# Rounding weight blocks two behind, and moving two small jobs behind the chain stages, in an attention-plus-MLP kernel

## The chip, the cores and the metric

The kernel runs on one core of a Trainium2 chip. The metric is the device time of one execution in microseconds (us); lower is better. Three runs of the kernel before gave 793.99, 795.82 and 796.3 us, with 795.82 us as the median. The profile and the trace come from one more execution, which took 794.06 us.

## The reference

A recurrent attention runs over 768 tokens for 4 batches of 8 heads with 40 elements each, and its output goes through a two-layer MLP (called moe in the code):

```python
for t in range(S):                       # S = 768, per batch and head
    y[t]  = r[t] @ state                 # state is 40 x 40
    Sa    = state @ a[t]
    state = state * w[t][:, None] - outer(Sa, b[t]) + outer(v[t], k[t])
x = y.transpose(0, 2, 1, 3).reshape(3072, 320)
h = x @ w_in                             # 320 x 2048, given as float64
g = where(h >= 1, h, where(h <= -1, 0, (h + 1)**2 / 4))
out = g @ w_out                          # 2048 x 320, given as float64
```

## The kernel before, in words

**Attention.** The 768 tokens are cut into 24 chunks (`c`) of 32 tokens, and the 32 heads into two halves (`hb`). One chunk and half has a generator `chain(c, hb)` with four stages, called one at a time by `stage(c, hb)`. The first stage multiplies scores with values and state (L519) and copies the result on ACT (L523). The second multiplies with the inverse of the chunk's triangular matrix (L529) and writes it back in four pieces on DVE (L536) and four on ACT (L540); the two engines swap PSUM tiles halfway, and the profile shows DVE's third piece waiting for ACT's pieces and ACT's third for DVE's. The third makes the new state and the output (L545 to L568), and the fourth the last product (L585, L587). Then `round_y` (L575 on ACT, L576 on POOL) splits the output into a rounded part and a rest in the tile `Y`.

**MLP.** When two chunks are done, `relayout` issues six DMAs on SP (L605 to L614) that bring `Y` into `X`, and the generator `moe` runs 64 tokens of all batches: `first` (L637, tile `ph`), `gate` (L647 and L648 on ACT, L650 on DVE, L653 on ACT, L654 on POOL) and `second` (L668). The first group starts in the fourth quarter of chunk 2's step.

**Weights.** The float64 weights are converted on the chip in 28 blocks: 12 of `w_in`, then 16 of `w_out`. `weights()` is a generator in which a block takes three pulls: in the first ACT writes the two tiles `x` (L751) and `low` (L755); in the second the block before is rounded by `split` (L771 on ACT, L772 on POOL or DVE); in the third DVE joins `x` and `low` (L759). `split(k)` also issues the load of raw block `k + 5` (L739) on SP's queue for `w_out`. Blocks of `w_out` have three places for `x` and one for `low`, all in `tiab`.

**Order.** The program is one hand-written order; each engine and each queue runs its own part of it in order. One step of the main loop (L923 on) handles a chunk in four quarters. Each quarter calls the stages that are ready, hands out turns and loads, and then calls `fill`, which interleaves six portions of MLP matmuls, of weight pulls (0.8 a portion in the first two steps, then 1) and of background work for later chunks (rows, pair products and inverses, with their own windows). In the second and fourth quarter, `shift` (two copies on ACT, L310) prepares the transposed columns that `turn` (L464, L467, L469 on DVE) takes up later. In those two quarters the order on ACT is: the two copies of `shift`, the fourth stage's `round_y`, then the four pieces L540 of the other half's second stage.

Of the kernel before, what the change touches and what calls it, by code (L numbers as in the profile page):

```python
# [55 lines left out]
def rwkv_moe_kernel(ctx: ExitStack, tc: tile.TileContext, r, k, v, w, a, b, w_in, w_out, ident_d, mask_d, out):  # L56
# [30 lines left out]
    tiab = const.tile([128, 16, 80], F32, name="tiab")  # L87
# [25 lines left out]
    pairs_f = pairs.rearrange("p m i -> p (m i)")  # L113
# [22 lines left out]
    def copy_rv(s, part, c, n=1):  # L136

        x, o = ((r, O_R), (v, O_V))[part]
        nc.sync.dma_start(
            scr[s][0 : NH * 128].rearrange("(h x) e -> h x e", x=128)[:, L * c : L * (c + n), o : o + D],  # L140
            x.rearrange("b h t e -> (b h) t e")[:, 128 * s + L * c : 128 * s + L * (c + n), :],
        )

    flat = lambda x: x.rearrange("p a e -> p (a e)")
# [227 lines left out]
    def adopt(s):  # L372

        drain("inv", s)
        W = lw[:, 1024:2048]
        nc.vector.transpose(tinv.rearrange("p c h i -> p i (c h)"), W.rearrange("p (a i) -> p i a", i=32))
        turned_out.add(s)
# [33 lines left out]
    def background(n):  # L411

        due = []
        for key in ("inv", "ab", "rows"):
            for s in range(1, NS):
                a, b = window(key, s)
                if a < n <= b:
                    drain(key, s - 1)
                    at = spent.setdefault((key, s), [0])
                    due.append((key, s, at, size[key] * (gone(n) - gone(a)) / (gone(b) - gone(a))))  # L420
        while True:
            due = [(k, s, at, to) for k, s, at, to in due if done[k] < s and at[0] < to]
            if not due:
                return
            key, _, at, _ = max(due, key=lambda x: x[3] - x[2][0])
            at[0] += next(back[key])
# [3 lines left out]
    def load_ti(c, hb):  # L430
        drain("rows", c // 4)
        tis[c, hb] = tih[hb]
        load_rows(tih[hb], c, 0, 200, 16 * hb, 16)
# [20 lines left out]
    def shift(c, hb):  # L454
        shift_rows(tis[c, hb])
# [15 lines left out]
    def scores(c, hb, parts=(0, 1)):  # L471
        u = 2 * c + hb
        for part in parts:
            (score_products, score_masks)[part](u)
# [29 lines left out]
    def chain(c, hb):  # L504
# [11 lines left out]
        for h in range(16):  # L516
            f, p = h % 2, h // 2
# [8 lines left out]
        for h in range(16):  # L526
            f, p = h % 2, h // 2
# [26 lines left out]
        for h in range(16):  # L554
            f = h % 2
# [18 lines left out]
        def round_y():  # L574
            nc.scalar.copy(yv[:, 0], yt)  # L575
            nc.gpsimd.tensor_sub(yv[:, 1], yt, yv[:, 0].bitcast(F32))  # L576

        yield
        if last:
            round_y()  # L580
            return
        psv = psum()[:, 0:256].rearrange("p (h x) -> p h x", x=32)
        for h in range(16):
            f, p = h % 2, h // 2
            nc.tensor.matmul(psv[er[f], p, :], lhsT=ss[er[f], p, :], rhs=pn[er[f], p, 0, 8:40], start=True, stop=True)  # L585
        for f in range(2):
# [1 line left out]
                out=cn[er[f], f::2, C_R : C_R + 32], in0=psv[er[f]], scalar=-1.0,  # L588
                in1=pr[er[f], :, 1, 39:40].broadcast_to([D, 8, 32]), op0=ALU.mult, op1=ALU.mult,
            )  # L590
        round_y()
        yield

    groups = [(t, 64) for t in range(0, S, 64)]
# [131 lines left out]
    def weight_tile(k, t):  # L726
        kind, j, i, _ = jobs[k]
        if kind:
            if w2_pool[j // 8 ^ 1] is None:
                open_w2(j // 8 ^ 1)  # L730
            return w2_pool[j // 8 ^ 1].tile([128, 2, 320], t, name=f"w2_{j}", tag=f"w2_{j}")
        return w1_tile(j, i, t)

    def raw_load(k):
        raws[k] = weight_tile(k, F32).rearrange("p b n -> p (b n)")
        x, at = raws[k].bitcast(I32), 0
        for src in jobs[k][3]:
            m = src.shape[0]
            (nc.sync if jobs[k][0] else nc.gpsimd).dma_start(x[at : at + m], src.bitcast(I32))  # L739
            at += m  # L740

    def weights():

        def start(k):
            m, n = sizes[k]
            words = raws[k][0:m]
            if jobs[k][0]:
                x, low = (flat(tiab)[0:m, n * i : n * i + n] for i in (k % 3, 3))
            else:
                x, low = (Xraw[y][0:m, n * i : n * i + n] for y, i in (((1, 1), (0, 0), (1, 0), (0, 1))[k % 4], (1 - k % 2, 2)))  # L750
            nc.scalar.activation(  # L751
                x, words.rearrange("p (n b) -> p n b", b=2)[:, :, 1], AF.Prelu, scale=2.0**-112, alpha=2.0**32
            )
            low = low.bitcast(U32)
            nc.scalar.activation(  # L755
                low, words.bitcast(U8).rearrange("p (n b) -> p n b", b=8)[:, :, 3], AF.Copy, bias=-15.5 / 32, scale=1.0 / 32
            )
            yield
            nc.vector.scalar_tensor_tensor(  # L759
                out=x.bitcast(U32), in0=x.bitcast(U32), scalar=3, in1=low,  # L760
                op0=ALU.logical_shift_left, op1=ALU.bitwise_or,
            )
            yield x

        def split(k, x):
            m, n = sizes[k]
            kind, j, i, _ = jobs[k]
            del raws[k]
            wt[kind, j, i] = new = weight_tile(k, F32R)
            hi, lo = (new[0:m, p] for p in range(2))  # L770
            nc.scalar.copy(hi, x)  # L771
            (nc.gpsimd if kind or k < 7 else nc.vector).tensor_sub(lo, x, hi.bitcast(F32))  # L772
            converted[0] = k + 1
            if (kind, i) == (0, 2):
                wb = new.bitcast(F32)
                for q in range(2):
                    nc.gpsimd.dma_start(wb[80:120, q], wb[40 * q : 40 * q + 40, 0])
            if 12 <= k + AHEAD < len(jobs):
                raw_load(k + AHEAD)

        late = None
        for k in range(len(jobs)):
            s = start(k)
            next(s)
            yield
            if late:
                split(*late)
            yield
            late = k, next(s)
            yield  # L790
        split(*late)

    def pull(gen, n=1):
        for _ in range(n):
            if next(gen, "end") == "end":
                return False
        return True
# [45 lines left out]
    load_cg(0, 1)  # L843
    for i in range(2):
        copy_rv(0, i, 1)
    gens = {}

    def stage(c, hb):

        if (c, hb) in gens:  # L850
            next(gens[c, hb], 0)

    def turn_1(j, part):
        early_evict(1, j, part, early_turn(1, j, part))
# [13 lines left out]
    at(14, lambda: load_ti(1, 0))  # L868
    at(38, lambda: scores(0, 0, (1,)))
    gens[0, 0] = chain(0, 0)  # L870
    at(40, lambda: stage(0, 0))
    for half in range(2):
        at(41 + half, lambda half=half: early_ab(1, half))
    at(58, lambda: shift(0, 1))
    i = 0
# [17 lines left out]
    def feed(cols):  # L893

        if not Xs:
            return
        owed[0] += cols * (not idle[0])
        while owed[0] > 0:
            d = next(mgen)
            owed[0] = 0 if d is None else owed[0] - d  # L900
            idle[0] = d is None

    def catch_up():

        for f in deferred:
            f()
        deferred.clear()

    def fill():

        catch_up()
        for k in range(6):
            feed(1280)
            if first:
                first.pop(0)()
            due[0] += PACE[now[0] >= 20]
            while due[0] > 0:
                pull(wgen)
                due[0] -= 1
            background(now[0] + 10 / SLOTS * (k + 1) / 6)  # L920
        now[0] += 10 / SLOTS

    for c in range(NC + 1):  # L923
        nxt = c + 1 < NC
        if c < NC:
            if c:
                gens[c, 0] = chain(c, 0)
            gens[c, 1] = chain(c, 1)
        stage(c - 1, 1)
        if c:  # L930
            stage(c, 0)
        if c < NC:
            if c and c % 4 == 0:
                adopt(c // 4)
            for j in (0, 1) if c else (2, 0, 1):
                turn(c, 1, j)
        fill()
        if nxt:
            shift(c + 1, 0)
        stage(c - 1, 1)  # L940
        stage(c, 0)
        if c < NC:
            scores(c, 1)
        if nxt:
            load_ti(c + 1, 1)
        if nxt:
            load_cg(c + 1, 0)
            turn(c + 1, 0, 2)
        fill()
        for g, (t0, nt) in enumerate(groups):  # L950
            if t0 + nt == 32 * c:
                Xs[g] = relayout(g)
                if idle[0]:
                    owed[0], idle[0] = -TRAIL * 3072, False
        if c == NC:
            break
        stage(c, 0)
        stage(c, 1)
        if nxt:
            for j in (0, 1):  # L960
                turn(c + 1, 0, j)
        fill()
        if nxt:
            shift(c + 1, 1)
        stage(c, 0)
        stage(c, 1)
        if c + 2 < NC:
            load_ti(c + 2, 0)
        if nxt:
            scores(c + 1, 0)  # L970
            load_cg(c + 1, 1)
            turn(c + 1, 1, 2)
        fill()
# [33 lines left out]
```

## Time and profile before

| what | value |
|---|---|
| median of three runs | 795.82 us |
| the profiled execution | 794.06 us |
| its span, from the first to the last instruction | 792.2 us |
| PE busy, share of the span | 679.2 us, 86% |
| DVE | 587.9 us, 74% |
| ACT | 479.6 us, 61% |
| POOL | 444.5 us, 56% |
| mean granted clock of TensorE | 0.910 |

PE is TensorE's matmuls, DVE VectorE, ACT ScalarE, POOL GpSimd, SP SyncE, which issues most DMAs. A wait is idle time of an engine ahead of an instruction, put down to what ended it. The shares are means over stretches with different limits: chunks 0 and 1 have no MLP work, the weight blocks are done by 183 us, and the last instruction of the attention lies near 745 us.

### The profile page before, as it was taken

Reading aid. Unit: us, or ns where it says so; the run is one execution under the profiler, and the core shown is the slowest. Engines: PE = TensorE matmul, PEld = TensorE weight load, DVE = VectorE, ACT = ScalarE, POOL = GpSimd, SP = SyncE. Lnnn points to the kernel's source line nnn. Section 1 sums busy time; section 2 is a strip of 40 time slices with the busy share of each in tenths; the row PEclk is TensorE's granted clock in tenths of the full one; section 3 lists DMA queues with packets and bytes.
Section 4 is the critical chain, followed back from the end, with each engine's and each line's share of the span. In section 5 each row is a group of like instructions: output and inputs, shape, how many; then the busy total and the mean of one; then the engine's idle time right before and its main releaser. Section 6 shows DMA issues by size and latency. Waiting matters only on the chain.

```text
span 792.2 us, 35505 instructions
## 1 busy us (share of the span) xinstructions
PE 679.2 (86%) x15360; PEld 624.1 (79%) x15360; DVE 587.9 (74%) x1329; ACT 479.6 (61%) x1016; POOL 444.5 (56%) x615
## 2 busy tenths in 40 slices
PE   4645557787799888899979899999999999999997
PEld 3534546676788777889878789889999999999996
DVE  6997888778778776987767988778877778776211
ACT  5636756666465565557657466565765666655544
POOL 1232989765236998558657677654476642222332
PEclk9765555889799998899989999999999999999999
DMA  8899966765866566675338564442443324330000
GB/s 299 211 208 188 222 188 181 203 160 145 175 161 171 145 147 142 146 193 110 93 85 189 139 173 94 116 86 45 98 86 83 77 59 96 74 86 20 33 22 18
DMA packets 180523, 102.35 MB, mean 129 GB/s; under 512 B 124760, under 2 KB 172056, under 8 KB 180368
## 3 DMA queue, kind: packets, MB, share of 16 engines
q1 hardware_dynamic: 175216, 83.53, 46.6%
q0 software_dynamic: 4992, 16.39, 7.5%
q8 instruction: 121, 1.98, 1.1%
q14 instruction: 34, 0.28, 0.1%
q10 hardware_dynamic: 160, 0.16, 0.1%
HBM read 70.88 MB, written 27.53 MB: 124 GB/s over the span
## 4 chain that ended last, share of the span: by engine, by line
PE 50%; DVE 9%; DMA 5%; POOL 5%; ACT 4%; issue 3%; SPq 1%; ACTq 0%; DVEq 0%; POOLq 0%
PE ph L637 17%; PE po L668 15%; PE p L556 4%; PE p L585 3%; PE p L545 3%; PE p L485 3%; PE p L529 2%; PE p L519 2%; DMA scr<-arena 2%; DMA tiab<-scr 1%; PE p L336 1%; DVE gt L650 1%; POOL lw L369 1%; POOL gl L654 1%; DVE cg L563 1%
## 5 line engine op out<-in xcount | busy, mean ns | idle before, releaser
L654 POOL TENSOR_TENSOR gl<-gt,gh 128x512 fp32r<-128x512 f32 x95 | 122.0, 1284 | 204.9 <-ACT gh L653 155.7
L637 PE MATMUL ph<-X,w 120*128 120x256 f32 x1536 | 221.3, 297 | 3.1 <-DMA X<-Y 2.8
L637 PEld LDWEIGHTS ph<-X,w 120*128 120x128 f32 x1536 | 199.6, 199 | 11.1 <-issue 3.1
L668 PE MATMUL po<-w,gh 128*128 128x320 f32 x768 | 136.1, 320 | 10.6 <-ACT gh L653 10.0
L668 PEld LDWEIGHTS po<-w,gh 128*128 128x128 f32 x768 | 118.2, 195 | 13.3 <-ACT gh L653 11.8
L653 ACT CAST gh<-gt 128x512 fp32r<-128x512 f32 x95 | 58.8, 619 | 112.4 <-DVE gt L650 103.5
L650 DVE SCALAR_TENSOR_TENSOR gt<-gt,ph 128x512 f32<-128x512 f32 x95 | 65.0, 684 | 79.5 <-ACT gt L648 74.9
L647 ACT ACTIVATE gt<-ph,half_c 128x512 f32<-128x512 f32 x95 | 65.3, 688 | 56.5 <-PE ph L637 55.9
L369 POOL TENSOR_TENSOR lw<-lw 128x31 f32<-128x31 f32 (+15 forms) x155 | 91.6, 591 | 8.4
L536 DVE SCALAR_TENSOR_TENSOR cg<-p,mask 32x128 f32<-32x128 f32 x192 | 55.2, 287 | 48.9 <-ACT cg L540 44.8
L363 POOL TENSOR_TENSOR lw<-lw 128x31 f32<-128x31 f32 (+15 forms) x155 | 81.3, 525 | 7.9
L497 DVE TENSOR_TENSOR cg<-p,mask 32x256 f32<-32x256 f32 x192 | 80.5, 419 | 3.5
L668 PE MATMUL po<-w,gl 128*128 128x320 f32 x384 | 76.0, 321 | 7.1 <-POOL gl L654 7.1
L563 DVE SCALAR_TENSOR_TENSOR cg<-p,pr 40x160 f32<-40x160 f32 x184 | 59.0, 321 | 15.7 <-PE p L556 13.7
L668 PEld LDWEIGHTS po<-w,gl 128*128 128x128 f32 x384 | 62.4, 195 | 9.7 <-POOL gl L654 9.6
L556 PE MATMUL p<-cg 128*64 128x72 f32 (+1 forms) x1536 | 64.4, 241 | 0.0
L648 ACT ACTIVATE gt<-gt 128x512 f32<-128x512 f32 x95 | 60.0, 632 | 3.1
L545 PE MATMUL p<-cg 128*40 128x40 f32 x1472 | 43.9, 218 | 20.1 <-ACT cg L540 19.5
L545 PEld LDWEIGHTS p<-cg 128*40 128x40 f32 x1472 | 37.0, 130 | 30.2 <-ACT cg L540 23.3
L540 ACT ACTIVATE cg<-p 32x160 f32<-32x160 f32 x192 | 56.7, 296 | 6.5 <-DVE cg L536 2.6
L556 PEld LDWEIGHTS p<-cg 128*64 128x64 f32 x1536 | 58.8, 150 | 0.4 <-issue 0.4
L587 DVE SCALAR_TENSOR_TENSOR cg<-p,pr 40x256 f32<-40x256 f32 x92 | 38.5, 418 | 13.5 <-PE p L585 12.8
(105 smaller groups left out, 1097.4 us busy)
## 6 DMA issues: line engine op xcount, KB each, us to landing
ti<-scr SPq DMA_DIRECT2D x96, 200.0 KB
scr<-arena POOLq DMA_DIRECT2D x16, 640.0 KB, 5.3
cg<-scr SPq DMA_DIRECT2D x96, 80.0 KB
X<-Y SPq DMA_DIRECT2D x36, 160.0 KB
scr<-wide SPq DMA_DIRECT2D x8, 640.0 KB
w<-in_moe_w_out_dram SPq DMA_DIRECT2D x16, 320.0 KB
tiab<-scr SPq DMA_DIRECT2D x28, 160.0 KB
cg<-scr SPq DMA_DIRECT2D x96, 40.0 KB
```

The costliest lines, as they stand in the source:

```text
L363: eng.tensor_mul(t3, W3[:, 0:n, j : j + 1].broadcast_to([128, n, m]), L3[:, j + 1 :, j].unsqueeze(1).broadcast_to([128, n, m]),)
L369: eng.tensor_sub(W3[:, 0:n, j + 1 :], W3[:, 0:n, j + 1 :], t3)
L497: nc.vector.tensor_tensor(out=cg[q, f::2, C_X : C_X + 64][:, 4 * i : 4 * i + 4].rearrange("p h (j x) -> p h j x", x=32), in0=ps[quarter(f, ...
L545: nc.tensor.matmul(pst[er[h % 2], h // 2, :], lhsT=cg[:, h, C_S : C_S + D], rhs=cg[:, h, C_G : C_G + D], start=True, stop=True)
L556: nc.tensor.matmul(psv[h // 8][64 * f : 64 * f + 64, h // 2 % 4, 0:n3], lhsT=cgw[:, h * CW + C_G : h * CW + C_G + 64], rhs=cg[:, h, C_R : ...
L563: nc.vector.scalar_tensor_tensor(out=cn[er[f], f::2, C_S : C_S + D][:, halves[i]], in0=psv[i][er[f], :, 32:72], scalar=-1.0, in1=pr[er[f], ...
L637: nc.tensor.matmul(phs[k % 2][:, n * j : n * j + n], lhsT=wt[0, f // 4, wi // 2][:, wi % 2, fs], rhs=Xs[g][:, xi, :], start=i == 0, stop=i ...
L647: nc.scalar.activation(gt, ph, AF.Relu, bias=half_c, scale=0.5)
L648: nc.scalar.activation(gt, gt, AF.Square)
L650: nc.vector.scalar_tensor_tensor(out=gt, in0=gt, scalar=1.0, in1=ph, op0=ALU.min, op1=ALU.max)
L654: nc.gpsimd.tensor_sub(gl, gt, gh.bitcast(F32))
L668: nc.tensor.matmul(pos[i], lhsT=x[:, ts_], rhs=w, start=q == 0 and k == 0, stop=end)
```

## The change

There are four edits. `split` runs two blocks behind the join, not one. To allow it, `w_out` blocks get a fourth place for `x` in `tiab`, and `low` moves to three places in `pairs_f`, a tile that the inverses use at other times. `round_y` is not called at the end of a chain but put on a list `rounds`, which `finish_rounds` empties behind the stages of a quarter. In the second and fourth quarter `shift` stands behind both stages instead of ahead of them.

```diff
 def chain(c, hb):
-            round_y()
+            rounds.append(round_y)
             return
...
-        round_y()
+        rounds.append(round_y)
         yield

 def weights():
-                x, low = (flat(tiab)[0:m, n * i : n * i + n] for i in (k % 3, 3))
+                x, low = (y[0:m, n * i : n * i + n] for y, i in ((flat(tiab), k % 4), (pairs_f, k % 3)))
...
-        late = None
+        late = []
         for k in range(len(jobs)):
             s = start(k)
             next(s)
             yield
-            if late:
-                split(*late)
+            if len(late) == 2:
+                split(*late.pop(0))
             yield
-            late = k, next(s)
+            late.append((k, next(s)))
             yield
-        split(*late)
+        for x in late:
+            split(*x)
+            yield

 # main loop
+    def finish_rounds():
+        for f in rounds:
+            f()
+        rounds.clear()
...
         stage(c - 1, 1)
         if c:
             stage(c, 0)
+        finish_rounds()
...
         fill()
+        stage(c - 1, 1)
+        stage(c, 0)
         if nxt:
             shift(c + 1, 0)
-        stage(c - 1, 1)
-        stage(c, 0)
+        finish_rounds()
...
         stage(c, 0)
         stage(c, 1)
+        finish_rounds()
...
         fill()
+        stage(c, 0)
+        stage(c, 1)
         if nxt:
             shift(c + 1, 1)
-        stage(c, 0)
-        stage(c, 1)
+        finish_rounds()
```

## Rows read from the trace of the kernel before

**Rows 1.** Busy time by stretch: stretch, length; us busy (instructions); granted clock, DMA share, GB/s.
```profile
65.00:142.00 77.00, 46.77 (x1288) 40.88 (x1284) 67.76 (x144) 53.23 (x120) 60.69 (x91) 0.59 0.87 190
142.00:182.00 40.00, 31.73 (x598) 28.12 (x592) 29.69 (x61) 26.79 (x60) 26.98 (x30) 0.89 0.79 194
182.00:340.00 158.00, 134.36 (x3031) 120.90 (x3031) 122.69 (x271) 93.33 (x203) 101.49 (x134) 0.90 0.67 155
340.00:520.00 180.00, 169.42 (x3986) 155.23 (x3986) 142.15 (x327) 112.68 (x247) 120.74 (x171) 0.98 0.55 128
520.00:792.00 272.00, 264.41 (x5340) 249.18 (x5336) 173.21 (x409) 161.06 (x339) 117.00 (x152) 0.99 0.28 63
```

**Rows 2.** Waits of DVE, 65 to 142 us: us in total, times, longest.
```profile
DVE cg L536 <- ACT cg L540: 2.9, 4, 1.5
DVE w L772 <- ACT w L771: 2.2, 3, 0.7
DVE tiab L759 <- ACT tiab L755: 1.1, 2, 0.6
```

**Rows 3.** Waits of ACT, 65 to 142 us.
```profile
ACT w L771 <- DVE X L759: 13.1, 8, 3.0
ACT tiab L755 <- DVE tiab L759: 4.3, 2, 2.6
```

**Rows 4.** Waits of DVE, 142 to 182 us.
```profile
DVE gt L650 <- ACT gt L648: 6.6, 3, 3.0
...
DVE cg L536 <- ACT cg L540: 0.9, 2, 0.4
```

**Rows 5.** Waits of ACT, 142 to 182 us.
```profile
ACT tiab L755 <- DVE tiab L759: 4.7, 3, 1.7
ACT arena L272 <- DMA scr<-arena: 3.6, 1, 3.6
```

**Rows 6.** ACT in order of time, a fourth quarter: start, us, what.
```profile
248.92 0.93 ACT L310 COPY ti<-ti 32x320 f32<-32x320 f32 x2
249.86 0.41 ACT L575 CAST Y<-yt 128x256 fp32r<-128x256 f32 x1
250.29 1.25 ACT L540 ACTIVATE cg<-p 32x160 f32<-32x160 f32 x4
251.56 0.69 ACT L647 ACTIVATE gt<-ph,half_c 128x512 f32<-128x512 f32 x1
252.28 0.63 ACT L648 ACTIVATE gt<-gt 128x512 f32<-128x512 f32 x1
```

**Rows 7.** DVE in order of time, the same quarter.
```profile
250.93 0.61 DVE L536 SCALAR_TENSOR_TENSOR cg<-p,mask 32x128 f32<-32x128 f32 x2 [1.30 <-ACT cg L540]
...
253.32 0.71 DVE L469 STREAM_TRANSPOSE pr<-ti 128x512 f32<-128x512 f32 x1
254.06 0.69 DVE L650 SCALAR_TENSOR_TENSOR gt<-gt,ph 128x512 f32<-128x512 f32 x1
```

**Rows 8.** Waits of DVE, 182 to 340 us, then 340 to 520 us.
```profile
DVE cg L536 <- ACT cg L540: 9.2, 8, 1.5
...
DVE cg L536 <- ACT cg L540: 16.2, 12, 3.3
```

**Rows 9.** The last raw load on SP, a wait on POOL, and block 26's start on ACT.
```profile
161.23 0.47 SPq L739 DMA_DIRECT2D w<-in_moe_w_out_dram  x1
...
165.71 1.30 POOL L654 TENSOR_TENSOR gl<-gt,gh 128x512 fp32r<-128x512 f32 x1 [0.30 <-DMA w<-in_moe_w_out_dram]
...
170.99 0.48 ACT L751 ACTIVATE tiab<-w 128x320 f32<-128x320 f32 x1
```

**Rows 10.** Chain of waits near 460 us; then SP and PE near 610 us in order of time.
```profile
459.56 4.19 DMA X<-Y
...
609.28 0.77 SPq L614 DMA_DIRECT2D X<-Y  x1
...
615.62 1.57 PE L637 MATMUL ph<-X,w 120*128 120x256 f32 x11
```

More of the change, by code (lines that the diff above doesn't have):

```diff
@@ L845, in rwkv_moe_kernel @@
         copy_rv(0, i, 1)
-    gens = {}
+    gens, rounds = {}, []
     def stage(c, hb):
```

## The prediction

> **What bounds the kernel now.** I began with the busy time by stretch [rows 1], because the page's means mix stages with different limits. From 520 us on PE is busy 264.4 of 272 us at a clock of 0.99: the end is set there by PE's own work, and nothing that the change touches there can pay. What happens earlier counts by how soon the program order reaches that state. In 340 to 520 us PE still has 10.6 us of idle time (180 less 169.4), in 182 to 340 us 23.6 us (158 less 134.4). From 65 to 142 us PE is busy 46.8 of 77 us and DVE 67.8, and DVE's waits in it that ACT ends through lines of this change come to only 6.2 us [rows 1, 2]. The rest of DVE's time without work there goes to gaps between instructions and to one wait for the first shifted columns.
>
> Next come the waits. In the weight stretch ACT waits 13.1 us in L771 and 4.3 us in L755 for DVE's join [rows 3]. These are waits of the engine that is ahead: most of it costs nothing, and only what comes back to DVE is on the path. Then the timelines of one fourth quarter [rows 6, 7]: ACT runs the two copies of shift and the rounding of Y from 248.92 to 250.27 us, only then L540, and DVE's third piece L536 stands 1.30 us until ACT's first two pieces are out. DVE has such a wait in 8 cases (9.2 us) before 340 us and in 12 cases (16.2 us) from there to 520 us [rows 8].
>
> **The change part by part.** The sum is made against the profiled execution, 794.06 us, whose span is 792.2 us; the 1.9 us around the span stay.
>
> *Weights, 65 to 142 us.* No instruction is added or dropped; each split comes three pulls later. The join that a split reads is then five pulls old instead of two, and low has three places, so ACT's waits of rows 3 go. DVE's gain is bounded by its own waits: 2.2 (L772) and 1.1 (L759) from the weights and 2.9 (L536) from the moved shift, 6.2 us at the most [rows 2]. Nothing excludes a loss, since POOL's subtractions move against DVE's joins. I take 5.0 and keep 0 and 6.2 as ends. The lag forces no pull on the MLP: by the code, some 57 pulls are done when its first group begins (2 x 24 x 0.8 + 18), split(k) now comes in pull 3k + 8, so 17 blocks are rounded where the group's first pair asks for 14.
>
> *Weights, 142 to 182 us.* Here ACT runs the gates too, and DVE waits 6.6 us in L650 for L648 [rows 4]. ACT's stalls in L755 that feed it are 4.7 us in three places [rows 5]. But two of the three are in fills that follow a shift, and there the copies and the rounding, 0.93 + 0.41 = 1.34 us [rows 6], now stand between L540 and the gate. So the stalls yield 4.7 - 2 x 1.34 = 2.0 us. With 0.9 us of L536 [rows 4] this is 2.9; I take 3.0. The 3.6 us that ACT waits for the store of the arena [rows 5] is a DMA's latency and stays. Ends: 0 and 6.6 + 0.9 = 7.5.
>
> *Shift and round_y.* In the quarter of rows 6 and 7, L540 could start at 248.92 us, and DVE's third piece would follow its second without the 1.30. Behind it DVE's row of work keeps its length: L469, which ended at 254.03, would end at 252.72. It needs the copies, which would end near 251.1, so they hide behind DVE's masks ahead of L469; if that cover were gone, DVE would wait up to 0.93 us. ACT does the same work in another order: L647 still starts at 251.56 and L648 ends at 252.91 us. L650, which needs both engines, starts near 252.95 instead of 254.06: 1.1 us gained of the 1.30, and ACT's lateness is what comes next. Where DVE itself is late there is no wait to remove, and ACT does its 1.34 us later than now. I cost this at nothing on average.
>
> In 182 to 340 us the 8 cases give 8 x 1.1 = 8.8 us. Some of these quarters are held by DMAs or by PE at its lower clock (0.90 of full on average [rows 1]), so I take three quarters: 6.5, with 0 and 9.2 as ends. In 340 to 520 us PE is 94% busy: most of the 16.2 us is hidden under matmuls, and PE's idle time of 10.6 us is the upper end. I take 3.0 by the nearer end, which is none. After 520 us the same edit removes waits that cost nothing.
>
> *Raw loads.* Each is issued one block later in SP's order. The load at 161.23 us is block 27's; in its place stands block 26's, which starts at 170.99: 9.8 us of lead. The profile has a landing of such a load at 165.7 us, 4.5 us after that issue [rows 9]. I cost this at nothing; without that lead, ACT's head of queue would wait the difference.
>
> *Given back.* Latency loops do not shrink with the engines' work: arena stores, loads of rows, Y into X. The 3.6 us of rows 5 is one of them and the 4.19 us of an X load in the chain of waits another [rows 10]. I take 4.0 us off, the mean of these two, with 0 and 8 (both in full) as ends.
>
> Sum: 5.0 + 3.0 + 6.5 + 3.0 - 4.0 = 13.5 us, 794.06 - 13.5 = 780.6 us. The median of the runs lies 1.8 us over the profiled execution, so the forecast in the runs' terms is 782 us. With the low ends of the gains and 8 given back it would be no better than before; with the high ends (6.2 + 7.5 + 9.2 + 10.6 = 33.5) it is 762.
>
> **The rivals.**
>
> *Half of it comes back.* What speaks for it: on ACT the 1.34 us stand ahead of the gate in every second and fourth quarter, and from 182 us on that gate is a loop of ACT and DVE. The weights' 8.0 us survive at half and the shift's 9.5 at a quarter, 6.4 us: 789 us. Against it: in the quarter worked out above the loop itself gets 1.1 us shorter.
>
> *A faster PE.* The granted clock is 0.90 in 182 to 340 us and 0.98 in 340 to 520 [rows 1], a mix of its two levels; a share of 0.10 missing out of 158 us means 31.6 us at 1.2 GHz, and 15.8 us of lost work. If fewer idle stretches bring half of it back, some 8 us come on top: 774 us. Against it: the waits on DMAs, which leave PE idle longest, stay.
>
> The Trainium skill (TensorE: Matmul & The Clock Gate, What's actually happening) says that the throttled state is the default and activity releases it. The rows agree in kind: the clock is 0.59 in the stretch where PE stands idle most, 0.99 where it does least [rows 1]. By that rule alone this rival would be the forecast.
>
> *Nothing moves.* DVE's waits are only shifted to L650 and the DMA loops take all of the weights' gain: 795 us. For it: ACT's order of work has the same length as before. Against it: DVE's own waits are 6.2 us where DVE is 88% busy, and that is a bound that the DMAs do not set.
>
> *Slower: Y comes late to X.* With PE busy throughout, shift and rounding stand behind L540, so the rounding of Y ends about 1.25 us later (the length of the four pieces L540 [rows 6]), then the six X DMAs and the first L637. Near 610 us the last X DMA is issued at 609.28, and PE takes X up at 615.62. At a landing time of 4.19 us [rows 10] that leaves 2.1 us. It decides from the point where the delay passes this slack: a landing over 5.1 us, or a fill that is 0.9 us shorter. The price would be PE idle in seven groups after 340 us, 1.25 us each plus about the same in matmuls at the lower clock, 17.5 us, against the 13.5 gained: 800 us. Against it: 2.1 us is more than 1.25.
>
> **How the numbers follow.** Forecast at 782 us (775 to 788): 0.55. Half comes back, 789: 0.17. A faster PE, 774 or below: 0.11. Nothing moves, 795: 0.10. Slower, 800: 0.07. About 0.3%, 2.4 us, is what a measurement of this kernel can tell from no change; the first three cases are faster than that: 0.83 faster, 0.10 same, 0.07 slower. The range 767 to 794 us leaves out the slower case, the upper part of no change and the farthest of a faster PE, some 0.18.
>
> **What would show each step.** Right: ACT has no wait left in L771 for L759 and none in L755; DVE's wait in L536 for L540 drops from 9.2 and 16.2 us to under 3 each in the same chunks; the end of the weight stretch comes 6 to 8 us earlier and the state in which PE has no idle time some 13 us earlier; the tail from there keeps its length. Wrong: DVE's wait in L650 grows by as much as L536 loses; POOL or SP stand ahead of X, and PE waits at L637; ACT waits at L751 for a raw block; L469 waits for the copies; or the gain at the end of the weight stretch is gone by 520 us.

## The result and the profile after

The changed kernel takes 789.27 us (median of 6 runs, 784.09 to 791.32) where the kernel before takes 796.46 us beside it: a ratio of 0.9905, 95% interval 0.9883 to 0.9927. Two further measurements of the same kernel gave 0.9897 [0.9858, 0.9935] and 0.9947 [0.992, 0.9974]. By these ratios it is 4 to 8 us faster. The forecast was 782 us, with 775 to 788 as its own range; what came lies in the wider range and has the size of the rival "half of it comes back", 789.

Profiles are of one execution each, and executions of one kernel spread over 7 us (these six) to 11 us (28 of the kernel before, below). The two profiled here, 794.06 us before and 791.32 us after, are only 2.7 us apart: the first lies 2.4 us under its median in this measurement, the second 2.1 us over. So the traces place waits and stretches, and the sum is taken from the medians.

Busy time by stretch, after, in the columns of [rows 1]:

```profile
65.00:142.00 77.00, 48.72 (x1312) 43.00 (x1312) 67.79 (x145) 52.53 (x122) 62.03 (x86) 0.62 0.88 184
142.00:182.00 40.00, 29.80 (x560) 26.50 (x560) 33.92 (x62) 26.69 (x60) 29.47 (x34) 0.87 0.84 212
182.00:340.00 158.00, 136.42 (x2984) 122.88 (x2984) 120.37 (x266) 89.55 (x198) 99.81 (x133) 0.87 0.66 151
340.00:520.00 180.00, 171.19 (x4066) 157.85 (x4063) 145.46 (x339) 112.58 (x252) 122.86 (x173) 0.98 0.56 130
520.00:792.00 272.00, 262.53 (x5294) 247.62 (x5292) 170.69 (x401) 158.24 (x337) 116.86 (x152) 0.99 0.28 63
```

In 65 to 142 us PE did more (48.72 us against 46.77) at nearly the same DVE time. POOL did less and was busier: 86 instructions in 62.03 us against 91 in 60.69.

A stretch between fixed times mixes two programs, so the next table cuts by work: each half of a chunk opens with a row of matmuls L519 on PE, and the lengths run from the first of one half (chunk,half) to that of another. The last two columns are ACT's waits at its copy L272 in 180 to 321 us: for the store of the arena (`store`), and all of its idle time ahead of that copy (`all`), which has the wait for DVE's scan L235 too.

```
                     0,1-2,1  2,1-4,0  4,0-8,0  8,0-15,0  15,0-23,1  store    all
before                 52.32    52.95   140.50    199.19     210.07    4.2   11.2
weights_only           49.09    53.26   141.24    200.08     209.72    4.2   11.2
before_pool_relief     52.79    49.19   143.48    200.25     209.86    4.3   10.8
before_inv_half        50.48    52.21   137.77    197.67     209.77    4.4   11.0
moves_only             51.83    52.63   142.96    198.80     208.85   11.4   12.8
after                  49.17    54.66   142.55    197.86     208.85    8.5   13.9
after_again            49.43    57.04   140.95    199.57     208.85   11.8   13.0
after_third            49.21    56.08   142.26    198.05     208.86   13.0   14.1
after_pool_relief      49.19    48.31   141.48    197.48     208.85   13.3   14.4
after_inv_half         46.91    47.91   138.11    193.91     208.90   12.4   15.5
after_long_window      47.29    52.06   142.00    194.54     208.85   11.7   13.1
shift_in_gate          49.81    50.80   140.61    200.48     208.80   11.8   13.2
gate_and_window        47.79    48.48   139.46    197.49     208.80   12.9   16.1
store_in_two           49.02    55.04   137.75    197.39     208.79   none    9.4
```

In the kernel before, chunk half 2,1 begins at 127.67 us, 4,0 at 180.61, 8,0 at 321.1 and 15,0 at 520.30. The first four kernels have the old order of shift and rounding, the other ten rows the new one; after_again and after_third are the changed kernel once more. The profile of after_again is of the longest of its six executions (794.18 us), so no reading rests on it alone. In the first pair, before and after, the change gains 3.2 us by 2,1, loses 1.7 by 4,0 and another 2.1 by 8,0, then gains 1.3 and 1.2.

One kernel's stretches vary too: over the three profiles of the changed kernel by 0.3, 2.4, 1.6 and 1.7 us in the first four columns. From 4,0 to 8,0 the old order with all of the inverses' work has 140.50 to 143.48 us, and the new one, with the store uncut, 139.46 to 142.96. So no gain is shown there, and a loss of 2.1 us isn't shown either.

ACT's waits in 65 to 142 us, after, against [rows 3]. The 13.1 us in L771 and the 4.3 us in L755 are gone, and L751 has a wait that it did not have, for POOL's subtraction L772:

```profile
ACT X L751 <- POOL w L772: 3.6, 1, 3.6
ACT tiab L751 <- POOL w L772: 3.3, 3, 1.8
```

DVE's waits after, first 182 to 340 us, then 340 to 520 us. L536, 9.2 and 16.2 us in [rows 8], has no wait for L540 in the first and 3.5 us in the second:

```profile
DVE gt L650 <- ACT gt L648: 12.2, 8, 2.5
DVE cg L563 <- PE p L556: 11.5, 8, 2.7
...
DVE gt L650 <- ACT gt L648: 11.1, 12, 1.8
DVE cg L563 <- PE p L556: 8.4, 9, 1.5
...
DVE cg L536 <- ACT cg L540: 3.5, 2, 2.7
```

The same waits before:

```profile
DVE cg L563 <- PE p L556: 7.4, 7, 2.2
DVE gt L650 <- ACT gt L648: 4.1, 5, 1.2
...
DVE gt L650 <- ACT gt L648: 8.9, 9, 1.8
...
DVE cg L563 <- PE p L556: 2.1, 4, 1.0
```

The waits of the three lines come to 9.2 + 16.2 + 4.1 + 8.9 + 7.4 + 2.1 = 47.9 us before and 0 + 3.5 + 12.2 + 11.1 + 11.5 + 8.4 = 46.7 after.

### The profile page after: what moved, and what is told of

It reads as the page before. It is cut to its first block, busy times and chain, and to the rows that moved or that the text cites. A ratio compares the mean times of both kernels' runs of the same rounds, so it can differ in the third digit from the quotient of the medians.

```text
span 789.5 us, 35564 instructions
## 1 busy us (share of the span) xinstructions
PE 680.1 (86%) x15360; PEld 626.2 (79%) x15360; DVE 590.6 (75%) x1329; ACT 472.6 (60%) x1016; POOL 449.7 (57%) x615
## 4 chain that ended last, share of the span: by engine, by line
PE 61%; DVE 12%; POOL 10%; issue 6%; ACT 6%; DMA 4%; SPq 0%; POOLq 0%; ACTq 0%; DVEq 0%
PE ph L637 20%; PE po L668 18%; PE p L556 5%; PE p L545 3%; PE p L585 3%; PE p L485 3%; PE p L519 3%; PE p L529 3%; POOL lw L369 2%; POOL lw L363 2%; DMA scr<-arena 2%; POOL w L772 2%; PE p L336 1%; DMA tiab<-scr 1%; POOL gl L654 1%
## 5 line engine op out<-in xcount | busy, mean ns | idle before, releaser
L637 PE MATMUL ph<-X,w 120*128 120x256 f32 x1536 | 224.7, 301 | 5.1 <-DMA X<-Y 3.7
L654 POOL TENSOR_TENSOR gl<-gt,gh 128x512 fp32r<-128x512 f32 x95 | 122.1, 1285 | 163.8 <-ACT gh L653 156.9
L637 PEld LDWEIGHTS ph<-X,w 120*128 120x128 f32 x1536 | 203.1, 202 | 12.7 <-issue 3.0
L650 DVE SCALAR_TENSOR_TENSOR gt<-gt,ph 128x512 f32<-128x512 f32 x95 | 65.0, 685 | 94.0 <-ACT gt L648 85.8
L647 ACT ACTIVATE gt<-ph,half_c 128x512 f32<-128x512 f32 x95 | 65.2, 687 | 54.6 <-PE ph L637 53.8
L369 POOL TENSOR_TENSOR lw<-lw 128x31 f32<-128x31 f32 (+15 forms) x155 | 88.9, 573 | 8.4
L363 POOL TENSOR_TENSOR lw<-lw 128x31 f32<-128x31 f32 (+15 forms) x155 | 87.1, 562 | 8.0
L563 DVE SCALAR_TENSOR_TENSOR cg<-p,pr 40x160 f32<-40x160 f32 x184 | 59.1, 321 | 34.0 <-PE p L556 31.7
L540 ACT ACTIVATE cg<-p 32x160 f32<-32x160 f32 x192 | 56.5, 295 | 38.0 <-DVE cg L536 24.3
L556 PE MATMUL p<-cg 128*64 128x72 f32 (+1 forms) x1536 | 64.5, 242 | 0.0
L576 POOL TENSOR_TENSOR Y<-yt,Y 128x256 fp32r<-128x256 f32 x48 | 36.0, 750 | 49.1 <-ACT Y L575 49.0
L536 DVE SCALAR_TENSOR_TENSOR cg<-p,mask 32x128 f32<-32x128 f32 x192 | 55.2, 288 | 9.5 <-ACT cg L540 3.9
L545 PE MATMUL p<-cg 128*40 128x40 f32 x1472 | 42.2, 218 | 12.5 <-ACT cg L540 12.5
```

What stands on the lines that cost most here:

```text
L363: eng.tensor_mul(t3, W3[:, 0:n, j : j + 1].broadcast_to([128, n, m]), L3[:, j + 1 :, j].unsqueeze(1).broadcast_to([128, n, m]),)
L369: eng.tensor_sub(W3[:, 0:n, j + 1 :], W3[:, 0:n, j + 1 :], t3)
L545: nc.tensor.matmul(pst[er[h % 2], h // 2, :], lhsT=cg[:, h, C_S : C_S + D], rhs=cg[:, h, C_G : C_G + D], start=True, stop=True)
L556: nc.tensor.matmul(psv[h // 8][64 * f : 64 * f + 64, h // 2 % 4, 0:n3], lhsT=cgw[:, h * CW + C_G : h * CW + C_G + 64], rhs=cg[:, h, C_R : ...
L563: nc.vector.scalar_tensor_tensor(out=cn[er[f], f::2, C_S : C_S + D][:, halves[i]], in0=psv[i][er[f], :, 32:72], scalar=-1.0, in1=pr[er[f], ...
L637: nc.tensor.matmul(phs[k % 2][:, n * j : n * j + n], lhsT=wt[0, f // 4, wi // 2][:, wi % 2, fs], rhs=Xs[g][:, xi, :], start=i == 0, stop=i ...
```

## The experiments

The first four ran on one chip with 28 runs of the kernel before (795.76 us).

**weights_only.** The kernel before with the later splits and their places; shift and rounding as before.

```diff
...
-            if late:
-                split(*late)
+            if len(late) == 2:
+                split(*late.pop(0))
...
```

> The weight part of the change alone (split two blocks behind, more places); shift and round_y stay ahead of the second stage. Theory P (POOL): in the changed kernel POOL has no idle time from about 78 to 150 us (inverse of set 1 and the blocks' subtractions), ACT now waits for it at L751, and what the weights save on ACT and DVE before 150 us is lost there. So this part alone gives 0 to 3 us (ratio 0.996 to 1.000), and ACT waits at L751 for POOL here too. Rival S (the sum of the prediction): the weights alone give about 8 us less half of the 4 given back, 6 us, ratio 0.992.

793.09 us, 0.996 [0.9935, 0.9986]: 3 us of gain. By 2,1 it has all that the whole change has there (49.09 us), so the weights alone make it. ACT's wait for POOL is there too:

```profile
ACT X L751 <- POOL w L772: 5.2, 3, 2.6
ACT tiab L751 <- POOL w L772: 5.0, 3, 3.0
```

**moves_only.** The changed kernel with the weights split one block behind, as before; shift and rounding stay moved.

```diff
...
-        late = []
+        late = None
...
-            if len(late) == 2:
-                split(*late.pop(0))
+            if late:
+                split(*late)
...
```

> The moved shift and round_y alone; the weight blocks are rounded one behind as before. Theory P: the rest of the gain, 4 to 7 us (0.991 to 0.995), nearly all of it by cutting DVE's waits at L536, and a chance share of it in which low-clock stretches fall. Rival S: 9.5 us less half of the 4 given back, 7.5 us, ratio 0.9905, with the gain in the chunks from 182 to 340 us. Rival N: in 182 to 340 us nothing is gained (in the one profile of the changed kernel the chunks 6 to 8 take as long as before), and the moves give under 3 us.

791.34 us, 0.9935 [0.9904, 0.9967]: 4 to 5 us. With the weights' 3 this is the whole within the intervals. The table shows one stretch in which the parts do hinder each other: from 2,1 to 4,0 each part alone is within 0.4 us of the kernel before (53.26 and 52.63 against 52.95), and both together take 54.66 to 57.04 us. From 4,0 to 8,0 nothing is gained, 142.96 us against 140.50, although DVE's wait in L536, 9.2 us between 182 and 340 us before, is gone. That is as rival N had it, though not its total of under 3 us.

**after_pool_relief and before_pool_relief.** The rest of a w_out block is written by ACT instead of POOL, as a copy of x and not as a difference: the rest is not computed, and ACT has 16 copies more.

```diff
-            (nc.gpsimd if kind or k < 7 else nc.vector).tensor_sub(lo, x, hi.bitcast(F32))
+            if kind:
+                nc.scalar.copy(lo, x)
+            else:
+                (nc.gpsimd if k < 7 else nc.vector).tensor_sub(lo, x, hi.bitcast(F32))
```

> The changed kernel, with the rest of the 16 w_out blocks no longer computed: ACT writes a copy of x in its place, so POOL is rid of 16 subtractions of 0.96 us, ACT has 16 copies of 0.45 us more. Theory P: POOL was the bound from 95 to 155 us, so ACT's waits at L751 for w_out blocks and the 4.6 us wait of PE for gl go, the first X comes earlier, and it gains 4 to 8 us on the changed kernel: ratio to the kernel before about 0.980 to 0.986. Rival D (DVE and ACT set the pace, POOL's lag is a shadow): no faster than the changed kernel, 0.988 to 0.993.

> The same relief of POOL on the kernel before (the rest of the w_out blocks is not computed; ACT copies instead). Theory P: before the change POOL's lag was hidden behind ACT's waits for DVE, so this gives little: 0 to 3 us, ratio 0.996 to 1.000. If it gains as much as on the changed kernel (5 us and more), POOL was the bound before too and the change did not make it so.

785.72 us, 0.9867 [0.9825, 0.991], on the changed kernel, and 792.5 us, 0.9959 [0.9935, 0.9983], on the old one. Relief of POOL is worth 3 us on the old kernel, at the upper end of what was expected. On the changed one it is some 3 us by the medians, less than the 4 to 8 of theory P, and the interval overlaps that of the changed kernel (0.9883 to 0.9927). Where it pays is the stretch 2,1 to 4,0: 48.31 and 49.19 us. The loss that the change has there (54.66) is gone with POOL's work. PE's waits of after_pool_relief in 130 to 182 us no longer name L654; in the changed kernel it was the largest of 142 to 182 us, and before it was 0.9 us. The largest wait of each, in the order named:

```profile
PE po L668 <- ACT gh L653: 5.1, 3, 2.9
```
```profile
PE po L668 <- POOL gl L654: 5.1, 3, 4.6
```
```profile
PE po L668 <- POOL gl L654: 0.9, 1, 0.9
```

**after_inv_half and before_inv_half.** Every second step of POOL's inverses is left out in every set after the first, its pulls kept.

```diff
             n, m = j + 1, 31 - j
+            if s and j % 2:
+                yield INV_STEP[j]
+                yield INV_STEP[j]
+                continue
```

> The changed kernel with the same steps of the inverses left out. Theory P: with POOL out of the way the change is worth more than its 7.5 us: 11 to 14 us under the kernel before with the same steps left out (0.975 to 0.982 to the kernel before), part of it in chunks 4 to 8, as the prediction had it. Rival D: still 6 to 8 us between the two, so it was not POOL that took the rest of the gain.

> The kernel before, with every second step of the inverses on POOL left out (the inverse is not the right one then); the pace of the rest is as it was. Theory P: POOL is the bound in chunks 6 and 7, where it is busy 90% of the time, so they shorten by 4 us or more, and the kernel gains 4 to 10 us (0.988 to 0.995). Rival D (DVE and ACT, or PE and its clock, are the bound): chunks 6 and 7 keep their length within 2 us and the ratio is 0.995 to 1.000.

776.19 us, 0.9746 [0.9716, 0.9777], and 784.92 us, 0.9859 [0.9833, 0.9885]: 8.7 us apart, between what the two theories gave. The table says where. From 0,1 to 4,0 the two are 102.69 - 94.82 = 7.9 us apart, near the 8.0 that the prediction had for the weights; with POOL's full work it is 105.27 - 103.83 = 1.4. From 4,0 to 8,0 both are 2.7 us and more shorter than with the full inverses, but the change still gains nothing (138.11 against 137.77): the inverses on POOL lengthen this stretch in both kernels, and are not what takes the change's gain there. The kernel before gains 11 us by its missing steps, more than either of its theories gave; chunks 6 and 7 have 3.3 us of it (67.7 to 64.5), where theory P asked for 4.

**after_again and after_long_window.** The changed kernel once more, and with the first set's inverse spread over a longer window, which is the set that POOL works on during the weights.

```diff
-    inv=[(2, 28), (55.5, 79), (85, 118), (121, 158), (161, 198)],
+    inv=[(2, 35), (55.5, 79), (85, 118), (121, 158), (161, 198)],
```

> The changed kernel unaltered, on the chip and in the rounds of the next three, and for a second profile. If the two parts add up (3.2 and 5.2 us), 0.989 to 0.991. The second profile should show again what the first did: chunks 6 and 7 (from 253 to 321 us) as long as before, within 1.5 us, though DVE no longer waits at L536.

> The changed kernel, with the inverse of set 1 spread over chunks 0 to 3.5 instead of 0 to 2.8; nothing is left out. Theory P: POOL's work between 78 and 150 us falls by a fifth and goes into 150 to 180 us, where POOL has idle time; ACT's waits at L751 for POOL and PE's wait for the first X shrink, and it is 2 to 4 us faster than the changed kernel (as with POOL's subtractions taken away, 3.0 us): 0.985 to 0.988. Rival D: same as the changed kernel, or slower by up to 3 us, since chunk 4 takes up the inverse later.

789.05 us, 0.9897 [0.9858, 0.9935], and 784.86 us, 0.9875 [0.9832, 0.9917]. The first is as expected, and in its profile chunks 6 and 7 take 68.9 us (67.7 before), within the 1.5 us set. The intervals of the two overlap. The stretches of the second go as POOL's part says, 47.29 and 52.06 us against 49.17 and 54.66, but the times do not show it beyond doubt.

**after_third, shift_in_gate and gate_and_window.** The changed kernel again; the same with the copies of shift inside the fill (and the third part of the turn behind it); and that with the longer window.

```diff
         for k in range(6):
             feed(1280)
+            if k == 4:
+                for f in in_gate:
+                    f()
+                in_gate.clear()
...
-            shift(c + 1, 0)
+            in_gate.append(lambda: shift(c + 1, 0))
...
-            turn(c + 1, 0, 2)
+            at_end.append(lambda: turn(c + 1, 0, 2))
```

> The changed kernel unaltered once more, beside the next two on the same chip, and for a third profile: 0.989 to 0.991. Theory P (POOL): from the second half of chunk 2 to chunk 4 it is again slower than the kernel before (52.95 us there; 54.7 and 57.0 in the first two profiles). Chance alone would put it below as often as above.

> The changed kernel with the two copies of shift issued behind the gate's first two ACT instructions (in the portion in which ACT waits for DVE's part of the gate), and the transposition that needs them at the end of that fill. Theory G (gate): in 182 to 520 us the wait moved from L536 to L650, because shift and rounding now stand ahead of L647 and L648; with shift out of their way DVE's wait at L650 for L648 falls from 12.2 to under 6 us in 182 to 340 us, and it is 2 to 5 us faster than the changed kernel (0.983 to 0.988). Rival L (latency of PE and of loads holds these chunks whatever ACT's order is): within 1.5 us of the changed kernel.

> Shift behind the gate and the inverse of set 1 spread to chunk 3.5, both on the changed kernel: a version that may beat both. If the two causes are separate their gains add: 2 to 5 us and 2.2 us, ratio 0.980 to 0.985. If theory G falls, 0.987 as with the longer window alone.

791.36 us, 0.9947 [0.992, 0.9974]; 786.89 us, 0.9865 [0.9834, 0.9896]; 782.37 us, 0.9828 [0.9795, 0.9861]. The first is over the 0.989 to 0.991 expected; its stretch from 2,1 to 4,0 is again longer than that of the kernel before (56.08 us), as theory P had it. The last beats both kernels, by 14.9 us the one before (797.25 us there) and by 9.0 us the changed one (791.36). The gain of shift_in_gate is of the size expected, but the mark by which theory G was to be known went the other way: DVE's wait in L650, 182 to 340 us, should have fallen from 12.2 us to under 6 and grew, and L563's fell instead (11.5 us before this edit). So why it is faster stays open.

```profile
DVE gt L650 <- ACT gt L648: 15.2, 10, 4.0
DVE cg L563 <- PE p L556: 7.6, 7, 2.9
```

**store_in_two.** The last two columns of the table separate old order and new one with no exception in the thirteen runs ahead of this one. This run takes the wait for the store away: three of the arena's four groups of columns leave as soon as they are written, from SP. For that the arena is laid out as two blocks (these lines are not shown).

```diff
+            nc.sync.dma_start(scr[s][0 : NH * 128, 80:200].rearrange("(p t) x -> p t x", t=L)[:, ts_, :], R)
...
-            nc.gpsimd.dma_start(scr[s][0 : NH * 128, 80:240].rearrange("(p t) x -> p t x", t=L)[:, ts_, :], R)
+            nc.gpsimd.dma_start(scr[s][0 : NH * 128, 200:240].rearrange("(p t) x -> p t x", t=L)[:, ts_, :], bt)
```

> The changed kernel, but the 160 columns of a prelude part's arena go out in two transfers: the first three of its four groups of 40 columns from SP as soon as the third is written, the last by POOL at the old place. ACT's copy L272 of the next part, which writes the second group, then waits only for a transfer that left some 5 us earlier. In the profiles, ACT's wait at L272 for that store, 180 to 321 us, is 4.2 to 4.3 us in every kernel that keeps shift and the rounding of Y at their old places, and 8.5 to 13.3 us in every one that moves them. Theory S: this wait is where the moves' gain went in chunks 4 to 7. Then it falls under 4 us here, the stretch from chunk 4 to chunk 8 (142.4 us in the changed kernel) comes under 139.5 us, and the time is 3 to 5 us below the changed kernel's: 784 to 787 us, ratio 0.985 to 0.988. Rival T: the wait is only ACT being early, with DVE or POOL bounding the stretch behind it. Then the wait falls just as much, the stretch keeps 141 to 143 us, DVE's waits in L650 and L563 or POOL's take its place, and the time is 789 to 791 us, ratio 0.990 to 0.994. Rival U: the packets of 160 and 480 bytes in place of 640 cost more than the wait: 792 us or more.

788.35 us, 0.9909 [0.9875, 0.9944]. The wait is gone, and the stretch from 4,0 to 8,0 is 137.75 us, under the 139.5 that theory S set and 3.2 to 4.8 us under the changed kernel's three profiles. The time isn't the 784 to 787 expected; the interval holds T's ratios and only touches S's. So one profile shows that the store lengthens this stretch; that the whole kernel gets faster without it is not shown. Nor is it shown how much of this belongs to the change: the kernel before waits 4.24 us for a store at 309 us as well, and the cut store was not run on it. ACT's waits at this copy (L273 there) in 180 to 321 us now have only DVE's scan L235:

```profile
ACT arena L273 <- DVE ld_w L235: 8.9, 4, 3.8
```

## Why the prediction was half right

**Weights, 65 to 142 us: 5.0 predicted, 3.2 found.** The 3.2 us are those up to 2,1 (127.67 us before); the rest of this window falls into the next stretch. ACT's waits for the join are gone as foretold. New is a wait of 6.9 us in L751, which is in no step of the prediction: the places that a split frees are freed by POOL, which runs its subtractions in order between the steps of an inverse. Of the 72 us from 78 to 150 us it waited 5.1 us before and 2.9 after. This took little ahead of 2,1: with POOL relieved or the inverses halved the pairs are 3.6 us apart there. What else kept it under 5.0 is not shown. The prediction said "Nothing excludes a loss, since POOL's subtractions move against DVE's joins" and put no price on it.

**Weights, 142 to 182 us: 3.0 predicted, a loss of 1.7 found (3.1 in after_third).** This is a step that failed, in its sign: it took ACT's stalls as the bound and gave POOL's queue no price. The chain of waits of the changed kernel shows how (start, us, engine, what):

```profile
121.76 2.04 PE p L556 x31
123.81 0.87 POOL w L772
...
126.68 0.73 POOL Y L576
127.41 0.82 POOL w L772
...
129.41 0.83 POOL w L772
130.23 1.33 POOL lw L369
...
147.08 0.77 POOL w L772
147.85 1.22 POOL gl L654
...
149.12 1.43 PE po L668 x4
```

PE reaches 2,1 4 us earlier (123.72 us against 127.67), but POOL does not follow: its L576, which the first X waits for, starts at 126.68 us where it started at 125.86 before, and its L654 comes behind it all. With POOL relieved the two kernels are 4.5 us apart from 0,1 to 4,0 (101.98 - 97.50), and with half the inverses 7.9: POOL's work takes the weights' gain. How it does so is shown less fully. weights_only has the same lag (2,1 at 125.51 us, L576 at 128.49) and PE's wait of 4.6 us at L654 as well, and lost only 0.3 us from 2,1 to 4,0. What the moves add to that in this stretch no run separates.

**Shift and rounding, 182 to 340 us: 6.5 predicted, no gain found (2.1 us lost in the first pair).** This is the term that failed most: one quarter's gain was multiplied by the cases, with no price on what waits next. The quarter of [rows 6, 7] did what was worked out for it, and more. DVE in that quarter, before (L536's first pieces), then DVE and ACT after:

```profile
249.04 0.58 DVE L536 SCALAR_TENSOR_TENSOR cg<-p,mask 32x128 f32<-32x128 f32 x2
```
```profile
248.51 1.23 DVE L536 SCALAR_TENSOR_TENSOR cg<-p,mask 32x128 f32<-32x128 f32 x4
...
252.28 0.69 DVE L650 SCALAR_TENSOR_TENSOR gt<-gt,ph 128x512 f32<-128x512 f32 x1
```
```profile
254.75 0.80 ACT L262 COPY wz<-ld_w 128x320 f32<-128x320 f32 x1
259.38 0.78 ACT L272 COPY arena<-ld_w 128x320 f32<-128x320 f32 x1 [3.84 <-DMA scr<-arena]
260.06 0.69 ACT L647 ACTIVATE gt<-ph,half_c 128x512 f32<-128x512 f32 x1
```

L536 runs without a break, and from it to L650 it is 3.77 us instead of 5.02: 1.25 us, where 1.1 was predicted. L650 stands 1.78 us earlier than the 254.06 of [rows 7], and L262 keeps that. Then the same stretch of ACT before:

```profile
256.54 0.83 ACT L262 COPY wz<-ld_w 128x320 f32<-128x320 f32 x1
258.94 0.78 ACT L272 COPY arena<-ld_w 128x320 f32<-128x320 f32 x1 [1.57 <-DVE ld_w L235]
259.62 0.68 ACT L647 ACTIVATE gt<-ph,half_c 128x512 f32<-128x512 f32 x1
```

L272 overwrites the arena, and the store of the part before has not landed: ACT waits 3.84 us and the next gate L647 starts 0.44 us later than before. All 1.8 us are lost in one wait, and 0.44 more. POOL's rows, before and after, show why the store is late:

```profile
250.34 0.74 POOL L576 TENSOR_TENSOR Y<-yt,Y 128x256 fp32r<-128x256 f32 x1
...
252.38 0.92 POOL L290 DMA_DIRECT2D scr<-arena  x1 [0.30 <-POOL arena L289]
```
```profile
251.07 0.73 POOL L576 TENSOR_TENSOR Y<-yt,Y 128x256 fp32r<-128x256 f32 x1 [1.35 <-ACT Y L575]
...
253.10 0.92 POOL L290 DMA_DIRECT2D scr<-arena  x1 [0.30 <-POOL arena L289]
```

L576 is POOL's half of the rounding. It now waits 1.35 us for ACT's half L575, which the change put behind L540 and the copies, and L290, which issues the store, stands behind L576 in POOL's order. So the change made the store late by its own edit. The prediction followed the rounding to X and had no step for what stands behind it on POOL. In 182 to 253 us this wait of POOL went from 0.8 to 5.9 us:

```profile
POOL Y L576 <- ACT Y L575: 0.8, 1, 0.8
```
```profile
POOL Y L576 <- ACT Y L575: 5.9, 3, 4.2
```

No run puts the rounding alone back, so what this costs the whole kernel is not shown.

The prediction named this loop and took 4.0 us off for all latency loops together. That was the wrong size. Between 180 and 321 us the wait for the store in L272 grew by 4.3 us here and by 7.2 to 9.1 in the other profiles of the new order (all but the last run's). Not all of that is new, since ACT waited for DVE's scan at the same copy before. ACT's waits there, before and after:

```profile
ACT arena L272 <- DVE ld_w L235: 6.9, 3, 3.9
...
ACT arena L272 <- DMA scr<-arena: 4.2, 1, 4.2
```
```profile
ACT arena L272 <- DMA scr<-arena: 8.5, 3, 4.3
...
ACT arena L272 <- DVE ld_w L235: 5.3, 2, 3.9
```

All of the idle time ahead of L272 is 10.8 to 11.2 us in the old order and 12.8 to 16.1 in the new one. In the changed kernel's three profiles that is 2 to 3 us more than the 11.2 before: a part of the 6.5 only. The prediction's own mark of error, that L650 grows by as much as L536 loses, is nearly there: 4.1 to 12.2 us, for 9.2 lost.

The Trainium skill (DMA: Bandwidth & Descriptors, Anatomy of one DMA) has about 2 us of a transfer from GpSimd as fixed, mostly the confirmation that the last byte has landed. By its formula 640 KB take 3.5 us, an estimate. From L290's start to L272's it is 6.3 us here (259.38 - 253.10), so the page's figure is too small for this store, among the other transfers that are under way.

**340 to 520 us: 3.0 predicted, 1.3 found** (199.19 to 197.86). With half the inverses it is 3.8 (197.67 to 193.91). The three profiles of the changed kernel spread over 1.7 us there, so the 1.3 are not firm.

**After 520 us: nothing predicted, 1.2 found.** The old order has 209.72 to 210.07 us from 15,0 to 23,1, the new one 208.79 to 208.90, in all fourteen profiles. moves_only has it and weights_only does not, so the moves make it. PE's row for that stretch, before and after:

```profile
520.30:730.40 210.10, 209.26 (x4864) 195.72 (x4861) 161.33 (x386) 131.99 (x287) 97.41 (x135) 1.00 0.34 75
```
```profile
518.80:727.60 208.80, 208.80 (x4858) 195.45 (x4856) 160.18 (x383) 130.21 (x287) 97.78 (x135) 1.00 0.34 75
```

PE had 0.84 us of idle time left in 210 and now has none; the rest is PE's own busy time. "Waits that cost nothing" was not quite so.

**Right:** the raw loads cost nothing (L751 never waits for a DMA in 65 to 185 us), L469 in that quarter does not wait for the copies, Y does not come later to X (PE's waits for a DMA at L637 behind 340 us are 2.8 us before and 2.9 after), and the clock stands at 0.907 over the run against 0.910, so that no faster PE helped.

**The rivals.** "Half of it comes back" has the size, by its number alone. Its mechanism, a loop of ACT and DVE through the gate, is half of what was seen (L650's growth); POOL's queue, which took the weights' part, and the arena's store, which took some of the shift's, it does not have. That the total came within the wider range is in part luck: from 0,1 to 8,0, where 14.5 us of gain were placed, the first pair has 245.77 and 246.38 us.

**Open.** The two profiles are 2.7 us apart, 1.9 of it in the table's stretches, and the medians 7.2; the other 4.5 us are within the spread of single executions and are not placed. The 4 to 5 us of moves_only are not placed either: its five stretches sum to 655.07 us, those of the kernel before to 655.03. Why shift_in_gate is faster is open too, and what the moves lose beside the store from 4,0 to 8,0.

## What to carry to other kernels

A wait that goes gives its time only as far as the next wait in the same loop: follow the quarter on, past the instruction that gets earlier, to the first one that waits for something that did not get earlier (here a store that must land before its buffer is written again), before multiplying by the number of cases. When a job is moved on one engine, follow its other half too: here POOL's part of the rounding, and the store behind it. When work is handed out later to free one engine, look at the engine that gives the buffers back, and count the idle time that its queue has in that very stretch. And cut the traces by a piece of work, not by the clock on the wall: the last stretch agrees to 0.1 us in the ten profiles of the new order, where totals of one kernel spread over 7 to 11. But check each stretch for its own spread: that from 2,1 to 4,0 varies by 2.4 us in three profiles of one kernel.

## What was not expected of the hardware

The same POOL multiplication takes three times as long when certain work of DVE falls beside it. L363 on 128x255 elements, the second time in one set's inverse, before and after (start, us, what):

```profile
110.66 0.64 POOL L363 TENSOR_TENSOR lw<-lw 128x255 f32<-128x255 f32 x1
```
```profile
112.20 1.97 POOL L363 TENSOR_TENSOR lw<-lw 128x255 f32<-128x255 f32 x1
```

In the changed kernel DVE runs these three beside it:

```profile
111.45 1.22 DVE L759 SCALAR_TENSOR_TENSOR X<-X 80x512 uint32<-80x512 uint32 x1
112.60 0.68 DVE L772 TENSOR_TENSOR w<-X,w 120x512 fp32r<-120x512 f32 x1
113.20 0.48 DVE L759 SCALAR_TENSOR_TENSOR tiab<-tiab,pairs 128x320 uint32<-128x320 uint32 x1
```

1.33 us more on POOL stand beside the 1.48 us from its start to the end of the last of the three (112.20 to 113.68). In both traces, 39 of the 74 instructions of the inverses that have L235, L759 or L772 of DVE beside them are over 0.3 us longer than the shortest of their shape; of the 546 others, with other work of DVE beside them or none, not one is. The Trainium skill (SBUF — State Buffer, SBUF: two separate sides) says that an instruction of DVE with two operands in SBUF and one of GpSimd take a shared port in turn, and the later one is blocked wholly. This trace agrees: the three read two operands in SBUF, the first began ahead of POOL's, and POOL is longer by about what was left of them. It may be a part of why 86 instructions of POOL cost more in 65 to 142 us than 91 did; no run here tells that apart.
